# Gated linear attention and a feed-forward layer: weights behind the third unit, five pair units, late turns by DMA, early copies on ScalarE, warm-up matmuls, patience 4

## Chip, cores, metric

One core of one Trainium2 chip. The metric is the device time of one execution in microseconds (us); lower is better. All times are from the chip. Medians are over all runs of a kernel.

## The reference, cut

For 4 batches x 8 heads, a 48 x 48 state is decayed row by row and updated at each of 768 positions; its output, gathered over heads, goes through a feed-forward layer with exact gelu.

```python
f = 1.0 / (1.0 + np.exp(-f_logit))
for t in range(S):                      # S = 768, D = 48
    state = f[:, :, t, :, None] * state + np.einsum('bhd,bhe->bhde', k[:, :, t], v[:, :, t])
    y[:, :, t] = np.einsum('bhd,bhde->bhe', q[:, :, t], state)
# x = y as (B*S, H*D) = (3072, 384)
h = x @ w_in                            # 384 -> 2048
out = (0.5 * h * (1.0 + erf(h / sqrt(2)))) @ w_out     # 2048 -> 384
```

## The kernel before

The positions are cut into 24 chunks of 128, two to a unit. ScalarE takes exp and ln of a unit's gates; TensorE sums them; VectorE scales keys and queries; TensorE turns (transposes) them, forms scores and state, and turns the outputs; a feed-forward group then handles the unit's 256 rows. Exp and gelu need different tables on ScalarE. The order of all instructions is made on the host by a list scheduler in the kernel, which prices every operation and each table switch; the device then runs each engine's list in that order.

```python
PATIENCE = 2.0
...
x = t     # when an operation could start; one that needs the other table is held back:
if o.table and act and o.table != act:
    x = max(t, min(t + 2 * TABLE, max([d.vis for d in o.deps] + [0.0]) + PATIENCE))
key = (int(x * 20 + 0.999), o.prio, o.seq)          # the smallest key is placed next
...
SIZES = [2] * 12
PAIRS = [0, 1, 2]          # "pair" units: rows interleaved, loads in runs of 384 bytes, not 192
LOADS = ["u0", "u1", "i0", "i1", "i2", "i3", "u2", "o0", "o1", "o2", "o3"]   # u: unit, i/o: weights
...
# a natural unit's loads: two halves, four tensors each; a pair unit's: four tensors, whole
# turn(): TensorE transposes keys and queries into a bank, VectorE copies them to kq
P.add("PE", 0.225, ..., name=f"Tk{n}"); P.add("PE", 0.225, ..., name=f"Tq{n}")
P.add("DVE", 0.61, ..., name=f"KQ{n}")
# outputs(): VectorE casts the output to yb, TensorE turns it, VectorE copies it to xT
P.add("DVE", 0.475, ..., name=f"YB{n}"); P.add("PE", 0.17, ..., name=f"XT{n}"); P.add("DVE", 0.27, ..., name=f"X{n}")
```

## Time and profile before

| | before |
|---|---|
| time, median of the first 3 runs | 203.02 us (202.73 to 205.19) |
| profiled span | 200.9 us |
| TensorE work priced at start-to-start times | 168.5 us |
| TensorE lost: 0 to 30, 30 to 122, after 122 us | 17.5, 8.8, 2.4 us |
| table loads of ScalarE | 29 after the first, 37.2 us |

"Lost" is the length of a stretch less the priced work in it, the prices being those of the prediction (whose own split has 8.7 and 2.6 us for the last two stretches). The lines of the profile that carry this are in the prediction.

### The profile page before, as it was taken

How to read it: one execution, taken by the hardware profiler on the slowest of the kernel's cores; microseconds unless marked ns; L12 is line 12 of the kernel's file. 1: busy time of each engine (PE TensorE's matmuls, PEld its weight loads, DVE VectorE, ACT ScalarE, POOL GpSimd, SP SyncE). 2: the span in 40 equal slices, each digit the busy share in tenths (PEclk: the TensorE clock that was granted, in tenths of full speed). 3: DMA queues.
4: the chain of work that ended last, by engine and by line, in shares of the span. 5: the costliest groups of instructions: out<-in, count | busy, mean ns of one | idle time of the engine just before them, and what ended most of it. 6: DMA issues, size and time to landing. Idle time of an engine off the chain costs nothing.

```text
span 200.9 us, 4982 instructions
## 1 busy us (share of the span) xinstructions
PE 182.2 (91%) x2010; PEld 141.7 (71%) x2010; DVE 103.7 (52%) x210; ACT 143.4 (71%) x243; POOL 52.4 (26%) x116
## 2 busy tenths in 40 slices
PE   0677989999989997997999999999999999999992
PEld 0446667687678687666868958967877969696961
DVE  4479661274386685887559728759778400000000
ACT  3642069989899979986999999769565828273740
POOL 7369236041133434105145411115303000000000
PEclk9999999999999999999999999999999999999999
DMA  6999999999899989989999993011001011110102
GB/s 155 261 224 172 175 269 189 182 220 202 181 216 195 182 203 186 203 177 210 182 197 214 191 214 96 3 39 39 3 0 65 16 42 39 38 44 11 68 0 78
DMA packets 93013, 27.04 MB, mean 135 GB/s; under 512 B 87872, under 2 KB 92480, under 8 KB 92992
## 3 DMA queue, kind: packets, MB, share of 16 engines
q1 hardware_dynamic: 90816, 23.60, 53.7%
q0 software_dynamic: 2176, 3.15, 9.4%
q8 instruction: 15, 0.25, 0.5%
q14 instruction: 6, 0.05, 0.1%
HBM read 25.17 MB, written 4.72 MB: 149 GB/s over the span
## 4 chain that ended last, share of the span: by engine, by line
PE 57%; ACT 20%; DMA 13%; SPq 3%; issue 3%; DVE 2%; POOL 1%; ACTq 0%; DVEq 0%
PE ps L667 25%; PE ps L652 20%; ACT L692 8%; ACT gT L657 6%; DMA fl<-in_f_logit_dram 5%; DMA win<-in_moe_w_in_dram 4%; DMA kt<-in_k_dram 3%; PE ps L444 3%; SPq L345 2%; ACT fl L368 2%; PE ps L535 2%; ACT lf L373 2%; PE ps L506 1%; ACT rg L400 1%; PE ps L385 1%
## 5 line engine op out<-in xcount | busy, mean ns | idle before, releaser
L652 PE MATMUL ps<-xT,win 128*128 128x256 bf16 x576 | 72.7, 277 | 3.1 <-ACT gT L657 3.0
L667 PE MATMUL ps<-wout,gT 128*128 128x384 bf16 x384 | 70.1, 326 | 0.4 <-DMA wout<-in_moe_w_out_dram 0.2
L652 PEld LDWEIGHTS <-win 128*128 128x128 bf16 x576 | 61.4, 115 | 6.0 <-issue 3.5
L657 ACT ACTIVATE gT<-ps 128x512 bf16<-128x512 f32 x96 | 53.1, 602 | 7.9 <-PE ps L652 5.6
L667 PEld LDWEIGHTS <-gT 128*128 128x128 bf16 x384 | 35.1, 97 | 21.3 <-ACT gT L657 1.3
L692 ACT ACT_TABLE_LOAD x29 | 37.2, 1283 | 0.5
L413 DVE TENSOR_TENSOR kp<-kt,rg 128x384 bf16<-128x384 f32 x24 | 13.9, 579 | 24.1 <-ACT rg L400 24.0
L671 ACT ACTIVATE osb<-ps 128x384 f32<-128x384 f32 x24 | 11.8, 493 | 20.2 <-PE ps L667 20.0
L456 DVE TENSOR_TENSOR am<-ps,mask 128x512 bf16<-128x512 f32 x36 | 23.1, 684 | 5.9 <-PE ps L535 5.8
L419 POOL CAST vb<-vt 128x384 bf16<-128x384 f32 x24 | 13.1, 554 | 43.7 <-DMA vt<-in_v_dram 43.4
L482 POOL TENSOR_TENSOR tn<-rr,gl 128x384 f32<-128x384 f32 x16 | 13.6, 850 | 41.5 <-DVE rr L480 38.7
L368 ACT ACTIVATE fl<-fl 128x768 f32<-128x768 f32 x12 | 10.3, 859 | 18.0 <-DMA fl<-in_f_logit_dram 17.9
L498 DVE CAST yb<-ps 128x384 bf16<-128x384 f32 x24 | 13.0, 553 | 11.9 <-PE ps L557 9.0
L449 DVE COPY kq<-ps 128x1024 bf16<-128x1024 bf16 x24 | 16.4, 685 | 3.3 <-PE ps L444 3.1
L487 POOL CAST sb<-tn 48x192 bf16<-48x192 f32 x40 | 15.3, 383 | 8.4 <-DVE tn L476 6.5
L400 ACT ACTIVATE rg<-ps 128x384 f32<-128x384 f32 x24 | 11.9, 495 | 6.8 <-PE ps L387 3.5
L416 DVE TENSOR_TENSOR qp<-qt,gt 128x384 bf16<-128x384 f32 x24 | 14.4, 601 | 0.2 <-ACT gt L402 0.2
L402 ACT ACTIVATE gt<-ps 128x384 f32<-128x384 f32 x24 | 11.9, 496 | 0.0
L444 PE MATMUL ps<-ident,kp 128*128 128x128 bf16 x96 | 10.2, 234 | 0.3 <-DVE kp L413 0.3
L456 DVE TENSOR_TENSOR am<-ps,maskp 128x512 bf16<-128x512 f32 x12 | 7.7, 685 | 5.4 <-PE ps L583 5.4
L444 PE MATMUL ps<-ident,qp 128*128 128x128 bf16 x96 | 10.2, 234 | 0.3 <-DVE qp L416 0.3
L373 ACT ACTIVATE lf<-fl 128x768 bf16<-128x768 f32 x12 | 10.1, 843 | 0.3
(58 smaller groups left out, 150.6 us busy)
## 6 DMA issues: line engine op xcount, KB each, us to landing
out_dram<-osb SPq DMA_DIRECT2D x24, 192.0 KB, 1.9
fl<-in_f_logit_dram SPq DMA_DIRECT2D x18, 192.0 KB, 3.8
kt<-in_k_dram SPq DMA_DIRECT2D x18, 192.0 KB, 3.7
qt<-in_q_dram SPq DMA_DIRECT2D x18, 192.0 KB, 3.8
vt<-in_v_dram SPq DMA_DIRECT2D x18, 192.0 KB, 3.7
win<-in_moe_w_in_dram POOLq DMA_DIRECT2D x4, 384.0 KB, 8.2
wout<-in_moe_w_out_dram POOLq DMA_DIRECT2D x4, 384.0 KB, 6.7
fl<-in_f_logit_dram SPq DMA_DIRECT2D x3, 384.0 KB, 4.2
```

The costliest lines, as they stand in the source:

```text
L368: P.add("ACT", 0.72, lambda: nc.scalar.activation(fl.t(), fl.t(), AF.Exp, scale=-1.0), rd=[("fl", n) for n in ns], wr=[("e", u)], bufs=[fl ...
L373: nc.scalar.activation(lf.t()[:, :, :, 0:D], v, AF.Ln, bias=1.0)
L400: P.add("ACT", 0.40, lambda g=gps[j], rg=rg: nc.scalar.activation(rg.t(), g.t()[:, 0:HD], AF.Exp, scale=-1.0), rd=[("g", n)], wr=[("rg", n ...
L416: P.add("DVE", 0.475, lambda y=y, gt=gt, j=j: nc.vector.tensor_tensor(y["qp"].t()[:, :, 0:D], half(u, x["qt"], j), gt.t().rearrange("p (h ...
L444: nc.tensor.transpose(tpv()[:, i, p, :], sr.t()[:, 2 * p:2 * p + 2, :], ident)
L449: P.add("DVE", 0.61, lambda tpv=tpv, kqv=kqv: nc.vector.tensor_copy(kqv(), tpv().rearrange("a i p (c t) -> a (i p) c t", c=2) if U[u]["pai ...
L456: P.add("DVE", 0.61, lambda hh=hh: nc.vector.tensor_tensor(ams[hh].t(), aps[hh].t().rearrange("p (h t) -> p h t", t=C), mk.unsqueeze(1).to ...
L487: P.add("POOL", 0.36, lambda hh=hh: nc.gpsimd.tensor_copy(sb.t()[64 * hh:64 * hh + D, :, D * hh:D * hh + D], tn.t()[64 * hh:64 * hh + D, : ...
L652: nc.tensor.matmul(hps.t()[:, i * tok:(i + 1) * tok], col(fo)[:, kk, :], xT.t()[:, kk, :], start=(kk == 0), stop=(kk == KO - 1))
L657: acts.append(P.add("ACT", 0.50, lambda u=u, hps=hps: nc.scalar.activation(gT.t()[:, u * pk:(u + 1) * pk, :].rearrange("p a b -> p (a b)") ...
L667: nc.tensor.matmul(op.t()[:, 0:d_model], gT.t()[:, fo, s_ * C:(s_ + 1) * C], wout[fo // 4][:, fo % 4, :], start=(fo == 0), stop=(fo == FO ...
L692: nc.scalar.preload_act_table_set({"exp": "natural_log_exp_and_others", "gelu": "gelu_and_others"}[o.table])
```

## The change

It means to keep TensorE fed: less turning on it, a warm clock early, fewer table switches, and a store of feed-forward work behind three units of attention. The core of the diff:

```diff
-PATIENCE = 2.0
+PATIENCE = 4.0
...
-                    x = max(t, min(t + 2 * TABLE, max([d.vis for d in o.deps] + [0.0]) + PATIENCE))
+                    x = max(t, min(t + 2 * TABLE, max([d.vis for d in o.deps] + [switched]) + PATIENCE))
...
-PAIRS = [0, 1, 2]
-LOADS = ["u0", "u1", "i0", "i1", "i2", "i3", "u2", "o0", "o1", "o2", "o3"]
+PAIRS = [0, 1, 2, 3, 4]
+EARLY = [0, 1]                      # their gate sums use the feed-forward part's banks
+HELP = [0, 1]                       # some of their copies go to ScalarE
+XDMA = [5, 6, 7, 8, 9, 10, 11]      # outputs turned by DMA
+KDMA = [9, 10, 11]                  # keys and queries turned by DMA
+WARM = 30.0
+LOADS = ['u0', 'u1', 'u2', 'i0', 'i1', 'i2', 'i3', 'o0', 'o1', 'o2', 'o3']
...
+            if i > 1 and order[i - 2][0] == "pool":     # in the plan, two weight loads in flight
+                gd.append(order[i - 2][1])
...
+                    P.add("DMA", 1.3, lambda ...: nc.sync.dma_start_transpose(
+                        kq.t()[:, i, :, j, :], sr.t().rearrange("p h d -> p (h d)")), ...
...
+            help_ = u in HELP and j == 0
+            P.add("ACT" if help_ else "DVE", 0.86 if help_ else 0.61, ..., name=f"KQ{n}")
...
+        if n // 2 in XDMA:
+            P.add("DMA", 1.3, lambda: nc.sync.dma_start_transpose(xT.t()[:, :, j * C:(j + 1) * C], yb.t()), ...
+            return
...
+            if o.opens is not None and o.start < WARM:   # fill TensorE's planned gaps
+                for _ in range(int((o.start - at - 0.25) / (0.11 if o.start < 10 else 0.06))):
+                    nc.tensor.matmul(o.opens.t()[:, 0:C], junk, junk, start=True, stop=True, ...)
```

Cut: new prices for many operations, the stores of pair units in two pieces, and a seed that is not used; comments in the diff are added. `switched` is the time of the last table switch: patience is now counted from that switch too, where it was counted from the operation's inputs alone.

More of the change, by code (lines that the diff above doesn't have):

```diff
@@ L1 @@
+import random
 from contextlib import ExitStack
@@ L17 @@
 TABLE = 1.28
-PATIENCE = 2.0
+PATIENCE = 4.0
+SPREAD, SEED = 0.0, 0
 class Slots:
@@ L59 @@
     __slots__ = ("eng", "dur", "fn", "bufs", "prio", "deps", "table", "start", "end", "vis", "seq", "name",
-                 "left", "outs", "inst", "chain")
+                 "left", "outs", "inst", "chain", "opens", "lag", "lat")
 class Plan:
@@ L68, in __init__, with add @@
         self.ops, self.w, self.r = [], {}, {}
-    def add(self, eng, dur, fn, rd=(), wr=(), bufs=(), prio=0.0, deps=(), table=None, name="", chain=None):
+    def add(self, eng, dur, fn, rd=(), wr=(), bufs=(), prio=0.0, deps=(), table=None, name="", chain=None, opens=None, lag=0.0, lat=None):
         o = Op()
@@ L73, in add @@
         o.start = o.end = o.vis = o.inst = None
-        o.chain = chain
+        o.chain, o.opens, o.lag = chain, opens, lag
+        o.lat = LAT[eng] if lat is None else lat
         o.seq = len(self.ops)
@@ L94, in run @@
         free["DMA"] = 1.8
-        act = None
+        rng = random.Random(SEED)
+        for o in self.ops:
+            if o.prio > -5:
+                o.prio += rng.uniform(-SPREAD, SPREAD)
+        act, switched = None, 0.0
         for o in self.ops:
@@ L108, in run @@
                 for d in o.deps:
-                    v = d.end if d.eng == o.eng and (o.eng != "DMA" or d is o.chain) else d.vis
+                    v = d.end if d.eng == o.eng and (o.eng != "DMA" or d is o.chain) else d.vis + o.lag
                     t = v if v > t else t
@@ L132, in run @@
             if o.table and o.table != act:
-                act = o.table
+                act, switched = o.table, t
                 d += TABLE
             o.start, o.end = t, t + d
-            o.vis = o.end + LAT[o.eng]
+            o.vis = o.end + o.lat
             free[o.eng] = o.end
@@ L314, in load @@
         prev = order[-1][1] if order else None
+        if prev is not None and order[-1][0] != eng:
+            prev.lat = 2.2
         gd = [gate] if gate is not None else []
@@ L318, in load @@
                 gd.append(pools[-1])
-            k = P.add("POOL", 0.8, None, deps=gd, prio=-1000 + i, name="i" + name)
+            if i > 1 and order[i - 2][0] == "pool":
+                gd.append(order[i - 2][1])
+            k = P.add("POOL", 0.8, None, deps=gd, prio=-1000 + i, name="i" + name, lat=1.0)
             o = P.add("DMA", dur, lambda: None, wr=wr, bufs=bufs, prio=i, name=name, chain=prev, deps=[k])
@@ L346 @@
                         out=x[nm].t().rearrange("p (h x) -> p h x", h=H), in_=srcp(a, m)),
-                        [(nm, 2 * m), (nm, 2 * m + 1)], [x[nm]], 1.2, f"{nm}{m}")
+                        [(nm, 2 * m), (nm, 2 * m + 1)], [x[nm]], 1.5, f"{nm}{m}")
             else:
@@ L355 @@
             load("pool", lambda m=m: nc.gpsimd.dma_start(out=win[m], in_=win_src[:, :, 512 * m:512 * m + 512]),
-                 [f"win{m}"], [], 2.2, what)
+                 [f"win{m}"], [], 2.56, what)
         else:
-            load("pool", lambda m=m: nc.gpsimd.dma_start(out=wout[m], in_=wo_src[m]), [f"wout{m}"], [], 2.2, what)
+            load("pool", lambda m=m: nc.gpsimd.dma_start(out=wout[m], in_=wo_src[m]), [f"wout{m}"], [], 2.15, what)
     def decays(u):
@@ L367, in decays @@
         flv = fl.t
-        P.add("ACT", 0.72, lambda: nc.scalar.activation(fl.t(), fl.t(), AF.Exp, scale=-1.0),
+        P.add("ACT", 0.84, lambda: nc.scalar.activation(fl.t(), fl.t(), AF.Exp, scale=-1.0),
               rd=[("fl", n) for n in ns], wr=[("e", u)], bufs=[fl], table="exp", prio=pr, name=f"E{u}")
@@ L373, in lnop @@
             nc.scalar.activation(lf.t()[:, :, :, 0:D], v, AF.Ln, bias=1.0)
-        P.add("ACT", 0.72, lnop, rd=[("e", u)] + z_lf, wr=[("lf", u)], bufs=[fl, lf], table="exp", prio=pr, name=f"L{u}")
-        gps = [s_m.new(), s_m.new()]
+        P.add("ACT", 0.84, lnop, rd=[("e", u)] + z_lf, wr=[("lf", u)], bufs=[fl, lf], table="exp", prio=pr, name=f"L{u}")
+        gps = [(s_fh if u in EARLY else s_m).new() for _ in range(2)]
         for j, n in enumerate(ns):
@@ L398, in decays @@
                   rd=[("lf", u)] + (["trip", "negp"] if pair else ["trin", "negcol"]), wr=[("g", n)],
-                  bufs=[lf, gps[j], gt, rg, y["kp"], y["qp"], gl], prio=pr, name=f"C{n}")
+                  bufs=[lf, gps[j], gt, rg, y["kp"], y["qp"], gl], prio=pr, opens=gps[j], name=f"C{n}")
             P.add("ACT", 0.40, lambda g=gps[j], rg=rg: nc.scalar.activation(rg.t(), g.t()[:, 0:HD], AF.Exp, scale=-1.0),
@@ L418, in decays @@
                 rd=[("gt", n), ("qt", n)] + z_qp, wr=[("qp", n)], bufs=[y["qp"], x["qt"], gt], prio=pr + 1, name=f"QP{n}")
-            P.add("POOL", 0.47, lambda y=y, j=j: nc.gpsimd.tensor_copy(
+            hv = u in HELP
+            P.add("ACT" if hv else "POOL", 0.40 if hv else 0.47, lambda y=y, j=j, hv=hv: (nc.scalar.copy if hv else nc.gpsimd.tensor_copy)(
                 y["vb"].t().rearrange("p (h d) -> p h d", h=H), half(u, x["vt"], j)),
@@ L423, with copier, store @@
     St = {}
+    def copier(act):
+        return nc.scalar.copy if act else nc.vector.tensor_copy
+    def store(n, osb):
+        r = out[n * C:(n + 1) * C, :]
+        if not U[n // 2]["pair"]:
+            nc.sync.dma_start(out=r, in_=osb.t())
+            return
+        for s in range(2):
+            nc.sync.dma_start(out=r.rearrange("(p j) m -> j p m", j=2)[s], in_=osb.t()[64 * s:64 * s + 64, :])
+    kqdeps = {n: [("kq", n)] for n in range(NCH)}
     def turn(u, kq):
@@ L430, in turn @@
             kp, qp = X[n]["kp"], X[n]["qp"]
+            if u in KDMA:
+                for i, (key, sr) in enumerate((("kp", kp), ("qp", qp))):
+                    P.add("DMA", 1.3, lambda i=i, sr=sr, j=j: nc.sync.dma_start_transpose(
+                        kq.t()[:, i, :, j, :], sr.t().rearrange("p h d -> p (h d)")),
+                        rd=[(key, n)], wr=[("tk" if i else "kq", n)], bufs=[sr, kq], prio=-6, lag=1.7, lat=0.4, name=f"{key}D{n}")
+                kqdeps[n] = [("tk", n), ("kq", n)]
+                continue
             tp = s_m.new()
@@ L445, in turn @@
             P.add("PE", 0.225, lambda kp=kp, trans=trans: trans(0, kp), rd=[("kp", n), "ident"], wr=[("tk", n)],
-                  bufs=[tp, kp, kq], prio=pr + 4, name=f"Tk{n}")
+                  bufs=[tp, kp, kq], prio=pr + 4, opens=tp, name=f"Tk{n}")
             P.add("PE", 0.225, lambda qp=qp, trans=trans: trans(1, qp), rd=[("qp", n), "ident"], wr=[("tq", n)],
                   bufs=[tp, qp], prio=pr + 4, name=f"Tq{n}")
-            P.add("DVE", 0.61, lambda tpv=tpv, kqv=kqv: nc.vector.tensor_copy(
+            help_ = u in HELP and j == 0
+            P.add("ACT" if help_ else "DVE", 0.86 if help_ else 0.61, lambda tpv=tpv, kqv=kqv, help_=help_: copier(help_)(
                 kqv(), tpv().rearrange("a i p (c t) -> a (i p) c t", c=2) if U[u]["pair"]
@@ L467, in carry @@
             P.add("PE", mmdur, mm, rd=mmrd, wr=[("sp", n)], bufs=[sp, tn] + mmbufs + ([] if first_c else [rr]),
-                  prio=pr + 3.5, name=f"S{n}")
+                  prio=pr + 3.5, opens=sp, name=f"S{n}")
         def spf():
@@ L491, in carry, with outputs @@
         return sb
-    def outputs(n, yp, pair):
+    def outputs(n, yp):
         g, j = grp[n]
@@ L496, in outputs @@
         pr = 10 * n
-        yb, xp = X[n]["yb"], s_m.new()
-        P.add("DVE", 0.475, lambda: nc.vector.tensor_copy(yb.t(), yp.t()[:, 0:HD]),
+        yb = X[n]["yb"]
+        help_ = n // 2 in HELP and n % 2 == 1
+        P.add("ACT" if help_ else "DVE", 0.40 if help_ else 0.475, lambda: copier(help_)(yb.t(), yp.t()[:, 0:HD]),
               rd=[("yp", n)], wr=[("yb", n)], bufs=[yp, yb], prio=pr + 2, name=f"YB{n}")
+        if n // 2 in XDMA:
+            P.add("DMA", 1.3, lambda: nc.sync.dma_start_transpose(xT.t()[:, :, j * C:(j + 1) * C], yb.t()),
+                  rd=[("yb", n)], wr=[("x", n)], bufs=[yb, xT], prio=-7, lag=1.7, lat=0.4, name=f"XD{n}")
+            return
+        xp = s_m.new()
         def xpv():
@@ L506, in xmm @@
                 nc.tensor.transpose(xpv()[:, i, :], yb.t()[:, i * C:(i + 1) * C], ident)
-        P.add("PE", 0.17, xmm, rd=[("yb", n), "ident"], wr=[("xp", n)], bufs=[yb, xp, xT], prio=pr + 1, name=f"XT{n}")
+        P.add("PE", 0.17, xmm, rd=[("yb", n), "ident"], wr=[("xp", n)], bufs=[yb, xp, xT], prio=pr + 1, opens=xp, name=f"XT{n}")
         def xcopy():
-            to = xT.t()[:, :, j * C:(j + 1) * C]
-            if pair:
-                nc.vector.tensor_copy(to.rearrange("a i (p s) -> a i s p", s=2), xpv().rearrange("a i (s p) -> a i s p", s=2))
-            else:
-                nc.vector.tensor_copy(to, xpv())
-        P.add("DVE", 0.27, xcopy, rd=[("xp", n)], wr=[("x", n)], bufs=[xp, xT], prio=pr + 1, name=f"X{n}")
+            copier(help_)(xT.t()[:, :, j * C:(j + 1) * C], xpv())
+        P.add("ACT" if help_ else "DVE", 0.39 if help_ else 0.27, xcopy, rd=[("xp", n)], wr=[("x", n)], bufs=[xp, xT], prio=pr + 1, name=f"X{n}")
     def inter(yp, lhs, osb, start):
@@ L536, in amm @@
                                          start=True, stop=True)
-            P.add("PE", 0.42, amm, rd=[("kq", n)], wr=[("ap", n)], bufs=[kq] + aps + ams, prio=pr + 3, name=f"A{n}")
+            P.add("PE", 0.36, amm, rd=kqdeps[n], wr=[("ap", n)], bufs=[kq] + aps + ams, prio=pr + 3, opens=aps[0], name=f"A{n}")
             mask_scores(aps, ams, ("am", n), f"AM{n}", ("ap", n), pr, mask, "mask")
@@ L559, in ymm @@
                                          skip_group_check=True)
-            P.add("PE", 0.36 + (0.175 if c else 0), ymm,
-                  rd=[("am", n, 0), ("am", n, 1), ("vb", n), ("kq", n)] + ([("sb", n - 1, 0), ("sb", n - 1, 1)] if c else []),
-                  wr=[("yp", n)], bufs=[yp, x["yb"], vb, kq] + ams + ([osb] if c else []), prio=pr + 2, name=f"Y{n}")
-            outputs(n, yp, False)
+            P.add("PE", 0.22 + (0.17 if c else 0), ymm,
+                  rd=[("am", n, 0), ("am", n, 1), ("vb", n)] + kqdeps[n] + ([("sb", n - 1, 0), ("sb", n - 1, 1)] if c else []),
+                  wr=[("yp", n)], bufs=[yp, x["yb"], vb, kq] + ams + ([osb] if c else []), prio=pr + 2, opens=yp, name=f"Y{n}")
+            outputs(n, yp)
     def attn_pair(u):
@@ L574, in attn_pair @@
         for jk in range(2):
-            aps = [s_ap.new(), s_ap.new()]
+            aps = [(s_fh if jk and u == 0 else s_ap).new() for _ in range(2)]
             ams.append([s_am.new(), s_am.new()])
@@ L586, in attn_pair @@
             P.add("PE", 0.45, amm, rd=[("kq", n) for n in ns], wr=[("ap", u, jk)], bufs=[kq] + aps + ams[-1],
-                  prio=pr + 3, name=f"A{u}.{jk}")
+                  prio=pr + 3, opens=aps[0], name=f"A{u}.{jk}")
             mask_scores(aps, ams[-1], ("am", u, jk), f"AM{u}.{jk}", ("ap", u, jk), pr,
@@ L599, in attn_pair @@
         P.add("PE", 0.5, smm, rd=[("kp", n) for n in ns] + [("vb", n) for n in ns],
-              wr=[("sp", n) for n in ns[:len(sps)]], bufs=sps + kps + vbs, prio=pr + 3.5, name=f"S{u}")
+              wr=[("sp", n) for n in ns[:len(sps)]], bufs=sps + kps + vbs, prio=pr + 3.5, opens=sps[0], name=f"S{u}")
         osb = St.get("sb") if n0 % nC else None
@@ L622, in attn_pair @@
               wr=[("yi", n) for n in ns] + ([("yp", n0)] if osb is None else []), bufs=yps + vbs + sum(ams, []) + [X[n]["yb"] for n in ns],
-              prio=pr + 2, name=f"YI{u}")
+              prio=pr + 2, opens=yps[0], name=f"YI{u}")
         for cc, n in enumerate(ns):
@@ L627, in attn_pair @@
                 continue
-            P.add("PE", 0.26, lambda cc=cc, o=o: inter(yps[cc], lambda p: kq.t()[:, 1, p, cc, :], o, False),
+            P.add("PE", 0.18, lambda cc=cc, o=o: inter(yps[cc], lambda p: kq.t()[:, 1, p, cc, :], o, False),
                   rd=[("yi", n), ("sb", n - 1, 0), ("sb", n - 1, 1)] + [("kq", m) for m in ns], wr=[("yp", n)],
@@ L631, in attn_pair @@
         for cc, n in enumerate(ns):
-            outputs(n, yps[cc], True)
+            outputs(n, yps[cc])
     def ffn_group(g, gate):
@@ L655, in ffn_group @@
                   rd=[("x", n) for n in ns] + [f"win{i}" for i in sorted({(u * pk + i) // 4 for i in range(pk)})],
-                  wr=[("h", g, u)], bufs=[xT, hps, gT], prio=pr, name=f"F1.{g}.{u}")
+                  wr=[("h", g, u)], bufs=[xT, hps, gT], prio=pr, opens=hps, name=f"F1.{g}.{u}")
             acts.append(P.add("ACT", 0.50, lambda u=u, hps=hps: nc.scalar.activation(
@@ L672, in ffn_group @@
                   rd=[("o", n)], wr=[("os", n)], bufs=[op, osb], prio=pr - 1000, name=f"O{n}")
-            P.add("DMA", 0.55, lambda n=n, osb=osb: nc.sync.dma_start(out=out[n * C:(n + 1) * C, :], in_=osb.t()),
-                  rd=[("os", n)], bufs=[osb], prio=-5, name=f"st{n}")
+            P.add("DMA", 1.0 if U[n // 2]["pair"] else 0.6, lambda n=n, osb=osb: store(n, osb),
+                  rd=[("os", n)], bufs=[osb], prio=-5, lag=4.0, name=f"st{n}")
         return acts
@@ L687 @@
     state = {}
+    junk = one.tile([C, C], BF16, name="junk")
+    nc.gpsimd.memset(junk, 0.0)
+    at = 0.9
     for o in P.placed:
+        if o.eng == "PE":
+            if o.opens is not None and o.start < WARM:
+                for _ in range(int((o.start - at - 0.25) / (0.11 if o.start < 10 else 0.06))):
+                    nc.tensor.matmul(o.opens.t()[:, 0:C], junk, junk, start=True, stop=True, skip_group_check=True)
+            at = o.end
         if o.table and state.get("t") != o.table:
```

## The prediction

> **What bounds the kernel now.** I read the page first, then the busy time by stretch, the groups of instructions, the chain of waits and the timeline of the first 30 us. On the page the rows to look at are the engines' shares and, in the 40 slices, TensorE beside ScalarE and the DMA.
>
> ```profile
> span 200.9 us, 4982 instructions
> PE 182.2 (91%) x2010; PEld 141.7 (71%) x2010; DVE 103.7 (52%) x210; ACT 143.4 (71%) x243; POOL 52.4 (26%) x116
> PE   0677989999989997997999999999999999999992
> ACT  3642069989899979986999999769565828273740
> DMA  6999999999899989989999993011001011110102
> ```
>
> TensorE is nearly full except in the first six slices (30 us) and the last. ScalarE is full from slice 7 to slice 25 and then has room. The DMA is full until slice 24 (about 122 us) and then almost idle. The busy time by stretch says the same in numbers; its columns are the length, then busy us of PE, PEld, DVE, ACT and POOL.
>
> ```profile
> 0.00:10.00 10.00, 3.29 (x27) 2.27 (x28) 4.53 (x27) 4.74 (x8) 5.80 (x30) 1.00 0.97 208
> 10.00:20.00 10.00, 7.60 (x118) 5.66 (x116) 8.84 (x16) 3.46 (x7) 7.79 (x13) 1.00 1.16 198
> 20.00:30.00 10.00, 8.73 (x124) 6.28 (x123) 6.34 (x12) 2.95 (x4) 2.81 (x7) 1.00 1.11 224
> ...
> 60.00:90.00 30.00, 28.30 (x336) 21.65 (x336) 21.56 (x42) 27.98 (x50) 9.14 (x18) 1.00 0.93 190
> 90.00:122.00 32.00, 30.46 (x355) 24.11 (x354) 20.26 (x39) 29.50 (x49) 10.70 (x21) 1.00 0.97 200
> 122.00:155.00 33.00, 32.62 (x401) 26.05 (x400) 25.49 (x48) 22.85 (x44) 8.12 (x15) 1.00 0.08 27
> 155.00:197.00 42.00, 42.00 (x341) 33.62 (x340) 2.93 (x6) 23.25 (x40) 0.00 (x0) 1.00 0.11 38
> ```
>
> From 155 us on nothing is left but four feed-forward groups, end to end. So the loads do not set the end (42 us of TensorE work are stored up when attention is done): what sets it is TensorE's total work plus whatever TensorE loses before 155 us.
>
> Busy time overstates the work, so I priced it by start-to-start times. The chain of waits has first-layer runs and second-layer runs of the feed-forward part without a gap (start, length, line, count):
>
> ```profile
> 39.10 1.31 PE ps L652 x12
> ...
> 47.37 1.30 PE ps L667 x8
> ```
>
> That is 0.109 us and 0.1625 us each; 576 and 384 of them make 62.8 + 62.4 = 125.2 us, 10.4 us for each of 12 groups. Attention at its warm start-to-start times (transposes 0.056, 96-column products 0.043, 48-column ones 0.0255, score products about 0.03, sums over 384 columns 0.16) comes to 43.3 us. Total work 168.5 us. The last matmul starts at 197.0, so TensorE loses about 29 us. By stretch, length less work: 0 to 30 us, 17.5 lost; 30 to 60, 2.1; 60 to 122, 6.6; 122 to 155, 2.2; after that 0.4. A tail of 3.9 us (last copy, last store) follows, and the measured time is 2.1 us above the profiled span.
>
> Two lines of the groups and the timeline explain the losses. Table loads of ScalarE:
>
> ```profile
> L692 ACT ACT_TABLE_LOAD x29 | 37.2, 1283 | 0.5
> ```
>
> Of these 29, 23 (29.5 us) fall between 30 and 122 us, where nine units arrive: about 2.5 loads a unit where two (to exp and back to gelu) would do. And the early matmuls run slow:
>
> ```profile
> 8.34 0.61 PE L444 MATMUL ps<-ident,kp 128*128 128x128 bf16 x4 [0.35 <-DVE kp L413]
> 8.80 0.61 PE L444 MATMUL ps<-ident,qp 128*128 128x128 bf16 x4
> ...
> 22.56 2.75 PE L652 MATMUL ps<-xT,win 128*128 128x256 bf16 x12
> ...
> 77.53 0.40 PE L444 MATMUL ps<-ident,kp 128*128 128x128 bf16 x4
> 77.76 0.39 PE L444 MATMUL ps<-ident,qp 128*128 128x128 bf16 x4
> ```
>
> Early, four transposes start 0.46 us after the four before them (115 ns each); later 0.23 us (57 ns). The first twelve first-layer matmuls take 2.75 us instead of 1.31. The row of granted clock shows full speed all the time, so it does not show this.
>
> **What the Trainium skill says.** (1) "TensorE: Matmul & The Clock Gate", Part 1: TensorE starts at half clock and reaches full clock after some 3.4 us of steady work, 107 against 56 ns for 128 columns. The trace agrees (115 and 57 ns); it stays slow until about 26 us, because early work is too sparse. (2) "ScalarE: Activation LUTs", What ACT_TABLE_LOAD costs: 1283 ns a load, and 2.66 us with a drain. The trace has the 1283 ns, but the next activation starts at once (27.89 + 1.28, next at 29.18), so I count 1.3. (3) "DMA: Bandwidth & Descriptors", Latency and other measured facts: a DMA transpose moves about 261 GB/s in one kernel; its section Anatomy gives a fixed cost of about 2 us for a transfer. No transpose by DMA is in this trace. (4) "Trainium Kernel Development and Optimization", Reading a trace: matmul busy time is a bad measure of nearness to the limit; the trace agrees, 182.2 busy against 168.5 priced.
>
> **The change, part by part.**
>
> *Outputs turned by DMA, units 5 to 11.* 14 chunks x 3 transposes x 0.056 = 2.35 us off TensorE; 14 copies of 351 ns off VectorE (52% busy, worth nothing by itself). *Keys and queries, units 9 to 11:* 6 chunks x 8 x 0.056 = 2.7 us off TensorE, 6 copies of 685 ns off VectorE. Together -5.0 us of TensorE work. The DMA takes 26 new transfers. I estimate 98 KB at the skill's 261 GB/s as 0.4 us of moving plus the fixed 2 us, so 2.5 to 5 us to land behind queued loads. A late output only delays a feed-forward group that waits anyway behind stored work. Late keys and queries are on the attention chain, but in the last units, where feed-forward work is stored up.
>
> *Pair units 3 and 4.* A pair unit costs TensorE more: summing its rows gives 4.8 us a unit against 3.2 for a natural one. Two more units: +3.2 us. Gain at the DMA: 12288 packets of 384 B took 21.8 us of 16 engines against 71.5 us for 73728 packets of 192 B, so 7.3 us against 7.9 us a unit. That is 1.3 us of a DMA that does not bind. The two-piece stores cost nothing visible.
>
> Net TensorE work: 168.5 - 5.0 + 3.2 = 166.7, **-1.8 us**. So most of the gain has to come from the losses.
>
> *Weights behind the third unit.* Twelve loads of about 1.8 us (21.8 us for 12) end near 24 us; the first weight tile is asked for when the third unit's keys land, near 19.5, and lands at 23 to 24. First-layer work then starts about where it does now (22.6), but warm, and with two groups turned, soon three. That is 31 us of feed-forward work with no exp unit to serve before unit 3 lands at about 41 us. Now, the second group's first layer is stretched from 32.6 to 47.1 us, with the tables changing at 27.9, 32.2, 34.4, 37.3 and 40.3.
>
> *Warm-up matmuls and early copies on ScalarE.* The junk fills gaps before 30 us, so the clock is up before the first real matmul at 6.4. It takes 1.4 us off the first 12 first-layer matmuls and 0.6 off the next 12, and shortens the early chains. ScalarE is idle there (11.2 of 30 us busy) and VectorE is the full one at 10 to 20 us (8.84 of 10), so about 12 copies of 0.4 to 0.9 us moved help. Against it: junk writes the bank that the next real step uses. Where that bank comes free late, junk runs late and delays the step; I allow 1 us.
>
> Sum for 0 to 30 us: by then nearly all attention of three units (3 x 4.8 less a tail, about 13.2) and some 3.5 us of feed-forward are done, 16.5 of 30: loss 13.5 instead of 17.5, less 1 for the junk. **-3 us.**
>
> *Patience 4 instead of 2 and three units in one exp stretch.* I expect 20 to 23 table loads instead of 29, so 8 to 11 us less on ScalarE, almost all before 125 us, where it is about 94% busy and TensorE loses 8.7 us. ScalarE stays close to full (a unit costs it about 4.1 us of exp work and 2.6 of tables, beside 0.65 of a group at 5.8 us: 10.5 us in a 10 us pace), so I take less than half of that loss away. **-3.5 us**, and **-0.6** after 122 us.
>
> Sum: 203.0 - 1.8 - 3 - 3.5 - 0.6 = **194.1, told as 194.0 us**.
>
> **The rivals.** (a) *Transposes by DMA come late.* The queue on SyncE is in order and the DMA is full to 122 us; transfers land in 3.7 us there already. If 26 transfers take 2 us of the DMA each, loads end 20 us or more later and TensorE, also in order, stops at steps planned for an earlier landing. For: DMA share 0.97. Against: 42 us of stored work at the end, an idle DMA after 122. It would make 197 to 201. (b) *The junk and the later weights cost more than the warm clock gives:* first-layer work starts at 28 instead of 23, +4 us: 198. For: weights took 8.7 us to land together. Against: two units' attention is the only TensorE work before that, and the third moves ahead. (c) *TensorE fills up completely from 24 us on:* the loss between 30 and 155 us drops to 3 or 4 us instead of about 7; 190 to 191. For: three groups in store; against: ScalarE's share.
>
> **Range and chances.** (c) gives the low end, 190.0, and (a) or (b) in part the high end, 199.0. The 2% mark is 199.0, so slower than that needs a rival in full: faster 0.86, same 0.11, slower 0.03.
>
> **What would show it right or wrong.** Right: TensorE matmuls without junk priced near 166.7 us; transposes at 57 ns before 20 us; first-layer work from 23 to 26 us, then TensorE full; 20 to 23 table loads; one exp stretch before the first gelu; pure feed-forward at the end still there (20 us or more). Wrong: the chain of waits led by the transposes' DMA after 60 us (rival a); a TensorE idle at 25 to 32 us behind weights (rival b); 27 or more table loads; attention of the last unit running to the end.

## The result

195.07 us (median of 4 runs, 194.0 to 195.96) beside 203.4 us (4 runs). Ratios here are the mean time of one kernel's fast runs over the mean of the other's in the same rounds, so not quite the ratio of the medians: **0.9575** (95% interval 0.9495 to 0.9656). The page of the kernel after, engines' shares and slices:

```profile
span 193.1 us, 5196 instructions
PE 181.1 (94%) x2117; PEld 143.1 (74%) x2117; DVE 93.4 (48%) x184; ACT 131.7 (68%) x237; POOL 51.0 (26%) x113
PE   7874999999999999999999999999996999999992
ACT  3786456716996888769878688718879967182741
PEclk9999699999999999999999999999999999999999
DMA  6999995899989997897887689777995635121102
L745 ACT ACT_TABLE_LOAD x15 | 19.2, 1283 | 0.3
```

TensorE is full from slice 7 almost to the end; ScalarE has room nearly everywhere; the DMA works to slice 32 (155 us) instead of 24. There are 15 table loads after the first instead of 29. New in the row of granted clock: a 6 in the fifth slice, 19 to 24 us (a slice is 4.8 us). Busy time by stretch (length, then PE, PEld, DVE, ACT, POOL, granted clock, DMA share, GB/s):

```profile
20.00:30.00 10.00, 9.45 (x168) 8.04 (x166) 7.18 (x13) 5.17 (x10) 4.96 (x9) 0.86 0.84 135
...
60.00:90.00 30.00, 30.00 (x414) 23.75 (x411) 21.95 (x41) 23.22 (x44) 11.39 (x22) 1.00 0.88 181
90.00:122.00 32.00, 31.86 (x380) 25.57 (x378) 23.68 (x42) 26.09 (x50) 10.81 (x20) 1.00 0.88 167
122.00:155.00 33.00, 31.15 (x304) 23.94 (x303) 12.92 (x22) 24.88 (x45) 6.72 (x13) 1.00 0.73 154
```

Early busy time includes the junk, so it proves nothing; from 60 to 122 us TensorE is busy 61.86 of 62 us (before, 58.76).

| priced as before | before | after | difference | predicted |
|---|---|---|---|---|
| TensorE work without junk | 168.5 | 166.8 | -1.7 | -1.8 |
| lost, 0 to 30 us | 17.5 | 17.3 | -0.2 | -3 |
| lost, 30 to 122 us | 8.8 | 1.7 | -7.0 | -3.5 |
| lost, after 122 us | 2.4 | 3.6 | +1.2 | -0.6 |
| tail of the span | 3.9 | 3.6 | -0.3 | - |

These add up to the span's -7.8 us within rounding. The total was nearly right; its parts were not.

**Why the first 30 us gave nothing.** The timeline shows it; PE, ACT and DVE lines of one stretch:

```profile
17.63 0.84 ACT L387 ACTIVATE fl<-fl 128x768 f32<-128x768 f32 x1 [0.17 <-DMA fl<-in_f_logit_dram]
18.38 0.99 ACT L491 COPY kq<-ps 128x1024 bf16<-128x1024 bf16 x1
19.42 1.54 PE L740 MATMUL ps<-junk 128*128 128x128 bf16 x13 [1.56 <-ACT kq L491]
20.76 0.63 PE L485 MATMUL ps<-ident,kp 128*128 128x128 bf16 x4
21.92 0.69 DVE L491 COPY kq<-ps 128x1024 bf16<-128x1024 bf16 x1 [4.41 <-PE ps L485]
26.22 0.82 PE L697 MATMUL ps<-xT,win 128*128 128x256 bf16 x6
```

The second unit's copy of turned keys and queries (L491) now belongs to ScalarE. It stands there behind the third unit's exp (L387), which waits for its load until 17.6 us. The Trainium skill calls ScalarE's queue strictly first in, first out ("TensorE: Matmul & The Clock Gate", the opening table), and the trace agrees: the copy ran next after that exp, while VectorE was idle for 4.41 us. TensorE idled 1.56 us for the bank. The 13 junk matmuls, which need the same bank, then ran at half clock, 115 ns each, ahead of the real transposes (0.63 us for four, the slow size); the granted clock was 0.50 from 19.4 to 22.8 us. That the idle time brought the clock down is not shown (see a2). First-layer work began at 26.2 us, not at 23 to 26, and 3.6 us later than in the kernel before (22.6).

**Why the end lost more.** The chain of waits late in the run, then TensorE's timeline:

```profile
...
139.62 3.94 DMA fl<-in_f_logit_dram
143.64 0.85 ACT fl L387
```

```profile
145.41 0.32 PE L404 MATMUL ps<-lf,trin 128*128 128x384 bf16 x1 [0.69 <-ACT lf L392]
147.32 2.13 PE L697 MATMUL ps<-xT,win 128*128 128x256 bf16 x18 [0.92 <-ACT gT L702]
```

The last unit's gates landed at 143.6 us, against 122 before. TensorE was waiting for them, then for the switch back to gelu. That is a mild form of rival (a).

### The profile page after: what moved, and what is told of

Its sections match the earlier page's. It is cut to its first block, busy times and chain, and to the rows that moved or that the text cites.

```text
span 193.1 us, 5196 instructions
## 1 busy us (share of the span) xinstructions
PE 181.1 (94%) x2117; PEld 143.1 (74%) x2117; DVE 93.4 (48%) x184; ACT 131.7 (68%) x237; POOL 51.0 (26%) x113
## 4 chain that ended last, share of the span: by engine, by line
PE 70%; DMA 11%; SPq 5%; ACT 4%; POOL 3%; issue 2%; DVE 2%; ACTq 0%; POOLq 0%
PE ps L712 27%; PE ps L697 27%; DMA fl<-in_f_logit_dram 6%; SPq L364 5%; PE ps L485 4%; DMA wout<-in_moe_w_out_dram 3%; PE ps L580 2%; DMA vt<-in_v_dram 2%; PE ps L564 1%; PE ps L602 1%; ACT L745 1%; PE ps L740 1%; POOL sb L529 1%; POOL tn L524 1%; PE ps L404 1%
## 5 line engine op out<-in xcount | busy, mean ns | idle before, releaser
L697 PE MATMUL ps<-xT,win 128*128 128x256 bf16 x576 | 70.0, 273 | 0.9 <-ACT gT L702 0.9
L702 ACT ACTIVATE gT<-ps 128x512 bf16<-128x512 f32 x96 | 54.6, 602 | 22.0 <-PE ps L697 19.4
L712 PE MATMUL ps<-wout,gT 128*128 128x384 bf16 x384 | 68.4, 326 | 0.2 <-DMA wout<-in_moe_w_out_dram 0.2
L712 PEld LDWEIGHTS <-gT 128*128 128x128 bf16 x384 | 35.9, 98 | 20.8 <-issue 0.3
L439 POOL CAST vb<-vt 128x384 bf16<-128x384 f32 x20 | 11.8, 600 | 68.9 <-DMA vt<-in_v_dram 68.7
L716 ACT ACTIVATE osb<-ps 128x384 f32<-128x384 f32 x24 | 11.7, 489 | 19.4 <-PE ps L712 19.1
L498 DVE TENSOR_TENSOR am<-ps,mask 128x512 bf16<-128x512 f32 x28 | 18.0, 684 | 12.9 <-PE ps L580 12.8
L435 DVE TENSOR_TENSOR qp<-qt,gt 128x384 bf16<-128x384 f32 x24 | 15.7, 653 | 0.0
L498 DVE TENSOR_TENSOR am<-ps,maskp 128x512 bf16<-128x512 f32 x20 | 12.8, 685 | 5.2 <-PE ps L628 5.1
L740 PE MATMUL ps<-junk 128*128 128x128 bf16 x113 | 11.3, 273 | 3.2 <-ACT kq L491 1.6
L491 DVE COPY kq<-ps 128x1024 bf16<-128x1024 bf16 x16 | 11.0, 686 | 6.7 <-PE ps L485 6.6
L387 ACT ACTIVATE fl<-fl 128x768 f32<-128x768 f32 x12 | 10.2, 849 | 5.1 <-DMA fl<-in_f_logit_dram 5.1
L740 PEld LDWEIGHTS <-junk 128*128 128x128 bf16 x113 | 9.9, 126 | 3.7 <-issue 2.5
```

The source lines that it names most:

```text
L435: P.add("DVE", 0.475, lambda y=y, gt=gt, j=j: nc.vector.tensor_tensor(y["qp"].t()[:, :, 0:D], half(u, x["qt"], j), gt.t().rearrange("p (h ...
L498: P.add("DVE", 0.61, lambda hh=hh: nc.vector.tensor_tensor(ams[hh].t(), aps[hh].t().rearrange("p (h t) -> p h t", t=C), mk.unsqueeze(1).to ...
L697: nc.tensor.matmul(hps.t()[:, i * tok:(i + 1) * tok], col(fo)[:, kk, :], xT.t()[:, kk, :], start=(kk == 0), stop=(kk == KO - 1))
L702: acts.append(P.add("ACT", 0.50, lambda u=u, hps=hps: nc.scalar.activation(gT.t()[:, u * pk:(u + 1) * pk, :].rearrange("p a b -> p (a b)") ...
L712: nc.tensor.matmul(op.t()[:, 0:d_model], gT.t()[:, fo, s_ * C:(s_ + 1) * C], wout[fo // 4][:, fo % 4, :], start=(fo == 0), stop=(fo == FO ...
L740: nc.tensor.matmul(o.opens.t()[:, 0:C], junk, junk, start=True, stop=True, skip_group_check=True)
```

## The experiments

There are two kinds. **Same plan:** the order of the host's scheduler is kept and one thing is altered in what is sent out. **New plan:** a setting is undone, and the scheduler makes a whole new order. A new plan tests a setting together with the order that it leads to, and the two cannot be told apart by it.

| run | kind | median us | ratio to before (95%) |
|---|---|---|---|
| the change | | 195.07 | 0.9575 (0.9495 to 0.9656) |
| a1_no_junk | same plan | 194.66 | 0.9568 (0.9526 to 0.9610) |
| a2_kq_on_vector (1 of 6 runs slow) | same plan | 193.40 | 0.9501 (0.9464 to 0.9539) |
| a3_weights_queued | same plan | 194.49 | 0.9567 (0.9536 to 0.9599) |
| d1_all (the three) | same plan | 193.93 | 0.9494 (0.9448 to 0.9540) |
| a4_more_tensor | same plan | 198.65 | 0.9782 (0.9742 to 0.9821) |
| b3_double_tables (failed: equals the change) | same plan | 195.26 | 0.9584 (0.9524 to 0.9644) |
| b5_slower_switch | same plan | 204.07 | 1.0045 (1.0018 to 1.0072) |
| b1_patience2 | new plan | 199.44 | 0.9782 (0.9733 to 0.9831) |
| b2_turn_on_tensor | new plan | 201.75 | 0.9880 (0.9816 to 0.9944) |
| c1_loads_old (11 of 20 runs slow; fast median 202.59) | new plan | 204.29 | 0.9960 (0.9924 to 0.9995) |
| c2_pairs3 | new plan | 210.40 | 1.0376 (1.0319 to 1.0433) |
| b4_before_patience4 (of the kernel before) | new plan | 207.39 | 1.0188 (1.0149 to 1.0227) |

All gave correct results. Differences in us below are differences of ratios times 203 us; for the change the mean of its two measurements, 0.958, is used.

**a1_no_junk.** Is the warm-up a help or in the way?

```diff
-WARM = 30.0
+WARM = 0.0
```

> The changed kernel with no warm-up matmuls; every real instruction keeps its place. Theory J (junk helps): without it the first 20 us run at 115 ns a transpose again, first-layer work starts 1 to 2 us later, 196 to 197 us. Rival (junk is on the path): in the trace of the changed kernel 13 + 8 junk matmuls of 115 ns stand in the chain of waits between 19.4 and 22.7 us, 2.4 us in all, because they wait for the same bank as the step they precede; then without them the time is the same or up to 1.5 us lower, 193.5 to 195 us.

194.66 us: the same. The clock is slow again early (granted 0.50 from 18.4 to 21.8 and from 25.3 to 28.7 us), but the junk is out of the chain, and TensorE's timeline has

```profile
24.59 0.90 PE L697 MATMUL ps<-xT,win 128*128 128x256 bf16 x6 [1.07 <-DMA win<-in_moe_w_in_dram]
```

First-layer work starts 1.6 us earlier and now waits for the weights. The rival holds. That the warm clock and the blocked bank cancel fits this, but the two were not taken apart.

**a2_kq_on_vector.** Is the copy's place on ScalarE what spoiled the start?

```diff
-            ... help_=help_: copier(help_)(kqv(), ...
+            ... help_=help_: copier(help_ and u == 0)(kqv(), ...
```

> The changed kernel with one copy given back: the second unit's first turned keys and queries are copied by VectorE again, all else in place. Theory: on ScalarE this copy stood behind the third unit's exp, which waited for its load until 17.6 us, while VectorE was idle from 17.5 to 21.9 us; TensorE idled and its clock fell to half. On VectorE the copy is done near 17.5, the 1.6 us wait of TensorE for it goes, the granted clock stays full at 20 to 25 us, and first-layer work starts 1 to 2 us earlier; end to end 0.5 to 2 us lower, 193 to 194.5. Rival: the weights' landing sets the start of feed-forward work, and nothing changes (195).

193.40 us, 0.8% (1.6 us) under the change, though the intervals touch. In the timeline TensorE's wait at that place is

```profile
18.30 1.30 PE L740 MATMUL ps<-junk 128*128 128x128 bf16 x13 [0.42 <-DVE kq L491]
25.09 0.82 PE L697 MATMUL ps<-xT,win 128*128 128x256 bf16 x6
```

0.42 instead of 1.56 us, and first-layer work starts at 25.1 instead of 26.2. So the wait behind the copy is shown. One expectation missed: the clock still fell, and for just as long. Busy time of the slow stretch, first of the change, then of this run (the third number from the end is the granted clock):

```profile
19.40:22.80 3.40, 3.38 (x31) 3.19 (x30) 0.69 (x1) 1.09 (x2) 2.68 (x5) 0.50 0.90 166
18.62:22.02 3.40, 3.40 (x37) 2.78 (x38) 0.69 (x1) 1.01 (x3) 2.10 (x3) 0.50 0.75 156
```

So the 1.56 us of idle time is not what brought the clock down, or not alone; its cause stays open. In a3 below, where no order of TensorE is altered, it was down from 17.5 to 24.3 us: the stretch differs from run to run.

**a3_weights_queued.** GpSimd hands out all eight weight loads in a row; in the change the fourth was handed out only at 29.6 us, behind GpSimd's other work.

```diff
+    at2 = next(o.start for o in P.placed if o.name == "ii1")
+    for o in P.placed:
+        if o.name[:2] in ("ii", "io") and o.start > at2:
+            o.start = at2
+    P.placed.sort(key=lambda o: (o.start, o.seq))
```

> The changed kernel with all eight weight loads handed out by GpSimd one after the other, as before the change, instead of spread behind its other work; all else in place. Theory: the fourth weight tile was handed out at 29.6 us behind GpSimd's own work and the DMA had a gap of 3 us there; closing the gap brings the last weights from 44.7 to about 40 us, the next unit's loads from 43.2 to about 38 us, the feed-forward work from then on 2 to 3.5 us earlier: 191.5 to 193. Rival: TensorE has other work then and the loads are not binding: within 0.5 us of 195.

194.49 us: the same. By the packets in the trace the last weight landed at 38.7 instead of 44.7 us, as meant, and it bought nothing: the rival holds.

**d1_all.** The three together.

> The three repairs together on the changed kernel's plan: no junk, the second unit's copy back on VectorE, weights handed out at once. Theory: each took something off the first 45 us (first-layer work at 24.6 instead of 26.2 us without junk; the copy 1.3 us earlier; weights all in by 38.7 instead of 44.7 us) and, as they sit one behind the other, they add where each alone hit the next limit: 190.5 to 193. Rival: the clock is cold without junk and the landing of the first weight tile at 23.8 us caps all of them: 193 to 194.5, no better than the copy alone (193.4).

193.93 us, 0.9494: no better than the copy alone (0.9501). Here too the rival holds, and the clock was cold as it says: twelve first-layer matmuls at 28 us still take the slow 2.76 us. Which of the two is the cap, the clock or the weights' landing, is open. With a2 it is the fastest version I ran; its interval touches that of the change.

**a4_more_tensor.** Does TensorE's total work set the end?

```diff
+            more = 3 if o.name[0] == "Y" and n.isdigit() and int(n) >= 10 else \
+                8 if o.name[0] == "A" and n.isdigit() and int(n) >= 18 else 0
+            for _ in range(more):
+                nc.tensor.matmul(o.opens.t()[:, 0:C], junk, junk, start=True, stop=True, ...)
```

> The changed kernel, same plan, with the TensorE work that the DMA turns took off put back as junk matmuls of the same size and number (3 before each of 14 output steps of units 5 to 11, 8 before each of 6 score steps of units 9 to 11: 90 x 0.056 = 5.0 us), while the turns stay on the DMA. Theory (TensorE's total work sets the end): 4.5 to 5.5 us longer, 199.5 to 200.6. Rival (after 90 us the end is set by waits for the DMA, work fits into gaps of about 3 to 4 us): 1 to 3 us longer, 196 to 198.

198.65 us, 4.1 us above the change (0.9782 less 0.958) for 5.0 us of work. Some 80% of added work shows, between the two expectations and nearer the first: TensorE's work is the bound in the main, with small gaps that take about a fifth. (The fifth is not sure: the interval of the change alone is 1.6 us wide to each side.)

**b2_turn_on_tensor.** The real undoing of the DMA turns.

```diff
-XDMA = [5, 6, 7, 8, 9, 10, 11]
-KDMA = [9, 10, 11]
+XDMA = []
+KDMA = []
```

> The changed kernel with all turns on TensorE (both lists of units for DMA turns empty); a new order is planned. Theory (TensorE's total work sets the end): 5.0 us more work, 198.5 to 201. The loads end near 122 us again instead of 154. Rival (the late loads that the turns cause eat the gain): 194 to 197.

201.75 us (the upper bound was 201): 6.1 us above the change. Together with a4, 4 us of these 6 are TensorE's work; the rest belongs to the new plan and cannot be split here. The last unit's exp starts at 125.1 us in this run's timeline, against 143.6 in the change: the late loads come with the turns by DMA. Landing times, from the issues of the kernel after (count, then us; the view gives no KB for transposes):

```profile
xT<-yb SPq DMA_TRANSPOSE x14, 3.1
kq<-kp SPq DMA_TRANSPOSE x6, 2.7
kq<-qp SPq DMA_TRANSPOSE x6, 2.5
```

**b3_double_tables, b5_slower_switch.** Does the time of the switches cost TensorE anything now? The first try sent each load twice:

```diff
-                nc.scalar.preload_act_table_set(...)
+                for _ in range(2):
+                    nc.scalar.preload_act_table_set(...)
```

> The changed kernel, same plan, each table load between exp and gelu sent twice: 29 or 30 loads instead of 15, 19 us more of ScalarE, nothing else moved. Theory T (a load's 1.28 us delays TensorE each time): 4 to 9 us longer, 199 to 204, TensorE loses 5 us or more between 30 and 122 us as in the kernel before. Rival (ScalarE has room at 68% busy, and the order alone filled TensorE): less than 2 us longer, 195 to 197.

The profile has `ACT_TABLE_LOAD x15`, as without it: the second of two equal loads never reached the chip. The run is the change once more, and I count it so. The repair puts a copy ahead of each switch:

```diff
+                nc.scalar.copy(spare, mask.unsqueeze(1).to_broadcast([C, 10, C]))
                 nc.scalar.preload_act_table_set(...)
```

> The test that the doubled table loads were meant to be (the compiler dropped the second of two equal loads, so 15 were run). The changed kernel, same plan, with a copy of 1280 elements by ScalarE (about 1.25 us) ahead of each of its 15 switches: as much more ScalarE time as some 15 more loads. Theory T (the time that switches take of ScalarE is what TensorE loses): 4 to 9 us longer than 195, TensorE loses 5 us or more between 30 and 122 us. Rival (ScalarE has room; what counts is in which order the groups stand): under 2 us longer, 195 to 197.

204.07 us, 9.4 us above the change. The groups of its profile show the dose:

```profile
L747 ACT ACT_TABLE_LOAD x15 | 19.2, 1283 | 0.3
L746 ACT CAST spare<-mask 128x1280 f32<-128x1280 bf16 x15 | 19.1, 1271 | 0.0
```

19.1 us more at the switches cost 9.4 us, almost 0.5 us for each, though ScalarE was only 68% busy. TensorE's loss from 30 to 122 us rose from 1.7 to 7.3 us, by the same pricing. So in one and the same order, time at the switches is dear. The change took 14 loads, 18 us, away from them.

**b1_patience2.** Patience back to 2 in the changed kernel.

```diff
-PATIENCE = 4.0
+PATIENCE = 2.0
```

> The changed kernel with patience 2 again, so its host-side planner makes a new order (28 table loads by its own count instead of 15 after the first). Theory T (fewer table loads are what fills TensorE between 30 and 122 us): TensorE loses 5 us or more there again instead of 1.7, time 198 to 200. Rival (the turns by DMA and the weights' place do it): table loads double but the time stays within 1.5 us, 194 to 196.5.

199.44 us, 4.1 us above the change; the page has 27 loads:

```profile
L745 ACT ACT_TABLE_LOAD x27 | 34.6, 1283 | 0.5
```

Theory T holds in its size; TensorE lost 5.4 us from 30 to 122 us.

**b4_before_patience4.** Patience 4 in the kernel before, alone. Its scheduler counts patience from the inputs only, not from the last switch too.

```diff
-PATIENCE = 2.0
+PATIENCE = 4.0
```

> The kernel before with patience 4 and nothing else; a new order is planned, with 22 switches instead of 30. Theory T (fewer loads mean less lost): 197 to 201. Rival (patience alone makes worse order here: groups wait for the table while nothing is stored up): 203 or longer, the loss of TensorE between 30 and 122 us not below 8 us.

207.39 us: 1.9% *slower* with 21 loads instead of 29:

```profile
L692 ACT ACT_TABLE_LOAD x21 | 26.9, 1283 | 0.3
```

TensorE lost 14.6 us from 30 to 122 us instead of 8.8. So fewer loads do not by themselves make a faster kernel: it depends on the order that they come with. I take it that TensorE had no other work while an exp waited for its turn, but did not test this, nor the changed rule of patience.

**c1_loads_old.** Weights ahead of the third unit again.

```diff
-LOADS = ['u0', 'u1', 'u2', 'i0', 'i1', 'i2', 'i3', 'o0', 'o1', 'o2', 'o3']
+LOADS = ['u0', 'u1', 'i0', 'i1', 'i2', 'i3', 'u2', 'o0', 'o1', 'o2', 'o3']
```

> The changed kernel with the first layer's weights ahead of the third unit again; a new order is planned. Theory (one long exp stretch and three stored groups start the good part): first-layer work starts earlier, near 20 us, but is cut by the third unit's exp; more table loads (20), TensorE loses 3 us or more between 30 and 60 us: 197 to 200. Rival (the order of the loads is worth nothing): 194 to 196.

204.29 us over 20 runs, 11 of them slow; the fast ones have a median of 202.59 us and the ratio 0.9960: worse than expected; nearly the whole gain is gone. Its profile fell in the slow state, so I read only counts from it (19 loads, as the plan has them) and leave open where its time went.

**c2_pairs3.** Three pair units again.

```diff
-PAIRS = [0, 1, 2, 3, 4]
+PAIRS = [0, 1, 2]
```

> The changed kernel with three pair units instead of five; a new order is planned. By the prediction's sum the two further pair units cost TensorE 3.2 us of work; if the new plan is as dense, the time falls to 191.5 to 193. Rival (the change's gain hangs on this one plan, and a neighbouring setting gives a less dense one): 196 to 201, with TensorE losing 5 us or more after 30 us though its work is 3 us less.

210.40 us, 16 us above the change and far outside both expectations, though TensorE's work is 3.3 us less (163.5). ScalarE's timeline at the fourth unit, first of the change, then of this run:

```profile
48.82 1.28 ACT L745 ACT_TABLE_LOAD   x1
50.11 0.84 ACT L387 ACTIVATE fl<-fl 128x768 f32<-128x768 f32 x1
```

```profile
54.60 0.60 ACT L702 ACTIVATE gT<-ps 128x512 bf16<-128x512 f32 x1 [0.16 <-PE ps L697]
55.21 1.28 ACT L745 ACT_TABLE_LOAD   x1
56.51 0.85 ACT L387 ACTIVATE fl<-fl 128x768 f32<-128x768 f32 x1
```

The fourth unit's exp starts 6.4 us later. By the packets in the trace, its gates are complete at 49.6 instead of 46.1 us: a pair unit's gates come whole with the first of four loads, a natural unit's second half only with the fifth of eight. By the landings of these loads (semaphores, which come after the last packet) it is 51.9 instead of 46.8 us, 5.1 of the 6.4 us. From 60 to 80 us TensorE then runs dry and its clock falls (busy time by stretch of this run; the change has 20.00 and 1.00 there):

```profile
60.00:80.00 20.00, 15.85 (x150) 10.95 (x150) 10.87 (x21) 12.92 (x25) 5.97 (x12) 0.79 0.96 194
```

That the later gates caused the later switch, and that the stored groups were used up by then, fits these numbers, but is argued from them and not tested alone. Nor does it cover the whole 16 us: priced as before, TensorE's loss after 122 us is also some 5.5 us larger than in the change, with a granted clock of 0.90 from 122 to 155 us, and why is open.

## Why the prediction was right, step by step

- **Bound by TensorE's work: right.** 5.0 us added gave 4.1 us (a4). One reading behind it is a little off: at 155 us in the kernel before 24 attention matmuls were still to come, the last at 159.2 us, so not quite "nothing is left but four feed-forward groups".
- **Net work -1.8 us: right** (-1.7 priced). But the two halves do not stand for what their settings are worth. The turns' -5.0 shows as 4 to 6 us (a4, b2). They landed in 2.5 to 3.1 us (medians), within the 2.5 to 5 us foreseen; the section from which the prediction has its fixed 2 us speaks of transfers handed out by GpSimd, and these went by SyncE's queue, so the agreement is no test of it. The pair units' "+3.2 us" is right as work (3.3 less without them) and wrong as a verdict: without them the kernel is 16 us slower. I named the packets' 1.3 us as their gain and missed that the gates arrive 3.5 us sooner (5.1 by the landing).
- **0 to 30 us, -3 us: wrong, -0.2.** The failed step is the sum of work done by 30 us: of "nearly all attention of three units" (13.2 us) some 10.5 were done, and of "some 3.5 us of feed-forward" 2.0 (18 first-layer matmuls at 0.109). One term is shown: "about 12 copies of 0.4 to 0.9 us moved help". One of them sat behind an exp that waited for a load; returning it gave 1.6 us end to end (a2), but only some 0.8 us more work before 30 us, and all three repairs together (d1) gave none there. The rest of the missing 2.8 us stays open. The junk, allowed 1 us, gained nothing (a1). The first weight tile landed as foreseen (23.8 us).
- **Patience, -3.5 us in the middle: half the size, and the mechanism right in the main.** I expected 20 to 23 loads and took "less than half of that loss away"; there were 15 loads and four fifths of the loss went. The mis-sized terms are the count of loads and ScalarE's room: I put it at 10.5 us of work in a 10 us pace, and it was busy 69.8 of the 92 us from 30 to 122 us, 76% (93% before). b5 prices the switches at 0.5 us each us, so 18 us fewer could pay for all 7.0 us, but b4 shows that this is no rule for another order, and the new rule of patience went untested.
- **After 122 us, -0.6: wrong sign, +1.2.** The last gates landed 21 us later than before. Rival (a) named this and gave it 197 to 201; stored work hid nearly all of it. That b2's last exp comes at 125.1 us supports it.
- **Rivals:** (c), TensorE full from 24 us on, came true in part, from about 30 us: the loss from 30 to 155 us was 4.8 us, between its 3 to 4 and my 7. The errors were +2.8 us at the start, -3.5 in the middle and +1.8 at the end; they cancelled, so that the total of 194.0 against 195.07 owes much to luck.
- **Signs named ahead:** work priced at 166.8 us (166.7 foreseen), one exp stretch before the first gelu (first switch at 25.1 us) and 23 us of pure feed-forward at the end (last attention matmul at 166.0) came true; 15 table loads instead of 20 to 23 and first-layer work at 26.2 us did not. Transposes had the warm length from 7.8 us on (0.40 us for four), but the slow one again at 20.8 us. None of the four signs of being wrong showed.

What stays open: how much of the 8.3 us belongs to each setting. Undone one at a time under a new plan, patience costs 4, the turns 6, the loads' order 8 and the pair units 16 us; that is 34 us for a gain of 8. The settings act through one plan. Not tested at all: the new rule of patience, the new prices, and the banks of the early gate sums.

## What to carry to other kernels

When the order comes from a scheduler, a setting has no worth of its own: test it inside a fixed order, by adding or taking one cost, and treat every re-planned variant as another kernel. Before moving work to an idle engine, look at what stands ahead of it in that engine's list and what that waits for: "idle" here meant "waiting for a load". And ask of a load's layout not only how fast the bytes come but which of them come first.

## What the Trainium skill lacked or had wrong

- "ScalarE: Activation LUTs" gives 2.66 us for a switch with its drain; here the load took 1.283 us and the next activation began at once (48.82 + 1.28, next at 50.11), and ScalarE's idle time before all 15 loads was 0.3 us together. No page that I read says that the second of two equal table loads is dropped (b3: 15 run, 30 asked for).
- "DMA: Bandwidth & Descriptors" has no time for a small transpose from SBUF to SBUF: here 3.1 us from issue to landing for 96 KB (384 columns) and 2.5 to 2.7 us for 128 KB (512 columns), beside loads.
- "TensorE: Matmul & The Clock Gate" has no word on warm-up matmuls that share a bank with the step that they precede: here 13 of them at 115 ns stood in the chain of waits, and leaving all of them out changed nothing (0.9568 against 0.958).
